# Eight of eighteen transposed blocks moved from DMA to TensorE in 20 attention steps, and one weight scaling moved from GpSimd to ScalarE

## The chip, the core and the metric

The kernel runs on one core of a Trainium2 chip. Its engines are TensorE (PE; PEld for its weight loads), VectorE (DVE), ScalarE (ACT), GpSimd (POOL) and SyncE (SP), which here only issues DMAs. Each engine works through its own queue in order. The metric is the device time of one launch in microseconds; lower is better. Each comparison gives the median of several runs.

## What is computed

Attention with a learned relative bias over 4 batches, 8 heads, 576 positions and head size 64, then two MoE-like dense layers on the 2304 tokens of width 512:

```python
scores = scale * q @ k.T + bias            # bias from log distances through a small MLP
attn = exp(scores - max) / (sum + 1e-9)
x = attn @ v                               # tokens x 512
h = x @ w_in                               # 512 -> 1024
ln = layernorm(h * softmax(h)) * g_ln
x = ln @ w_out                             # 1024 -> 512
gate, val = sigmoid(x @ w_gate), x @ w_val # 512 -> 1536
out = (gate * val) @ w_out2                # 1536 -> 512
```

All products run in float16 on TensorE with each operand split into a high half (the value rounded to float16) and a low half (what the rounding left), so that three float16 products make up one of nearly float32.

## The kernel before

**Attention steps.** The attention is cut into 72 steps (`ticks`). A step takes one pair of heads and 128 query rows (64 of each of two batches in the "M" blocks) against all 576 keys. The first 16 steps are the first block of batches 0 and 1, steps 16 to 19 their "M" block. The loop at the end of the listing runs over t and sends out, for each t, pieces of several steps:

- `a_qk(t)` (L543 to L558): scores on TensorE, into one PSUM tile `score`.
- `a_soft(t)`: VectorE adds the bias and takes the row maximum (L577), ScalarE takes the exponential with its row sum (L584).
- `a_split(t-1)`: the probabilities `pp` (float32, 2 heads x 576) are cast to float16, the high half, by ScalarE (L595) or, in every fourth step, by VectorE (L593); GpSimd subtracts to get the low half (L596 for 512 columns, L598 for the remaining 64); then one DMA issued by SP (L601) transposes the whole tile `p16`, 18 blocks of 128x128, into `pt`, so that the keys lie on the partitions. The trace calls the tile `p16` by the name p.
- `a_pv(t-4)`: TensorE multiplies the blocks of `pt` with V (L620, 28 matmuls; 56 in an "M" step). `a_x` and `a_xt` scale by the row sums and transpose the result for the first MoE.

The rings that bear on it: `p16` has 2 buffers until the first MoE's pools open and 3 after that (`NP160`, `NP16`); `p` and `pt` have 3, then 4. The PSUM pool "m" has 4 buffers, which the bias tiles, K and Q transposes, `a_xt` and the first MoE share.

**Side work.** Beside the steps run small pieces of side work, five for each t at first, then three: decoding, measuring and splitting of the first MoE's weights (`w1_steps`: L183 to L192, L717, L697 to L699), the bias tables for the later blocks (L403, L456, L476, L482, stored to `bias_d`), and then the first MoE itself (L767 to L832). After some 87 pieces, at about t = 17, `open_moe` runs, and from the t after that TensorE's order is as the code writes it (`tc.manual_schedule`); ahead of that, and on the other engines, a planner places the instructions by estimated times, the attention's with a higher priority.

**Second MoE.** Its three weight matrices are decoded (L183 to L188), and each block of 128x512 goes through `split_w`: GpSimd multiplies by a power of two into `w2tmp` (L695, two buffers), ScalarE casts the high half (L698), GpSimd subtracts to the low half (L699). The third matrix (12 blocks) can start when `w2_scale_out` has found its scale (L1148), and its halves are used by `second_out` (L1372). Beside this VectorE makes sums of blocks of the first two matrices (`w2_sums`, L1228) for the products that follow (L1304), and `gate_val` (L1342 to L1348, with L1209 and L1210) runs the gates of the first two groups of tokens.

## Time and profile before

| | us |
|---|---|
| median of 3 runs | 1077.29 (1076.18 to 1077.48) |
| the profiled execution, its own time | 1073.33 |
| its span, first to last instruction | 1071.6 |
| TensorE busy | 898.8 (84%) |
| VectorE busy | 769.3 (72%) |
| ScalarE busy | 618.9 (58%) |
| GpSimd busy | 426.4 (40%) |

The attention steps start at 72 us and end at about 570 us. Steps 0 to 19 take until about 250 us. From 570 to about 790 us the second MoE's weights are made ready beside the last tiles of the first MoE and the first two groups of the second; from 809 us on only products of the second MoE are left. In the rows below, "x" is the count, times are us from the start of the span unless marked ns, "[1.41 <-ACT ...]" is the idle time of the engine ahead of the instruction and what ended it, and 128x512 f16<-128x512 f32 is the shape of the output and of the input.

### The profile page before, as it was taken

The page shows a single profiled execution, that of the slowest core. Times are in us where ns is not written, and L with a number is a line of the kernel's source. Part 1 is how long each engine was busy: PE and PEld are TensorE (multiplying, and loading weights), DVE is VectorE, ACT ScalarE, POOL GpSimd, SP SyncE. Part 2 cuts the span into 40 slices and gives each one's busy share as a digit, 9 for nine tenths or more (in the row PEclk, how much of TensorE's full clock was granted, in tenths as well). Part 3 has the DMA queues.
Part 4 walks back from the last instruction along what each step waited for, and adds up shares of the span by engine and source line. Part 5 has one row for each costly group of instructions (what it writes and reads, how often), then busy time and mean ns, then how long its engine had stood idle before and what let it go on. Part 6 is the DMA issues. An engine that isn't in the chain of part 4 may idle for free.

```text
span 1071.6 us, 23952 instructions
## 1 busy us (share of the span) xinstructions
PE 898.8 (84%) x9566; PEld 634.6 (59%) x9566; DVE 769.3 (72%) x1556; ACT 618.9 (58%) x1283; POOL 426.4 (40%) x386
## 2 busy tenths in 40 slices
PE   2656465668888789989998887798999999999998
PEld 2534344455665566667665664345577856866873
DVE  6879989885576676667664999999954762871760
ACT  4787684767677797778873677744342322331331
POOL 3357555565566666455640487567000000000000
PEclk9656675568899999999999999998999999999999
DMA  7878999899889899999964555500110010001001
GB/s 226 286 231 201 219 242 274 201 239 197 171 177 204 181 196 200 194 205 204 162 123 152 165 158 186 168 24 17 40 40 20 1 60 20 2 1 41 2 1 40
DMA packets 256576, 146.54 MB, mean 137 GB/s; under 512 B 215376, under 2 KB 230992, under 8 KB 256464
## 3 DMA queue, kind: packets, MB, share of 16 engines
q1 hardware_dynamic: 253888, 143.18, 56.4%
q0 software_dynamic: 2048, 1.58, 0.6%
q8 instruction: 75, 1.23, 0.5%
q10 hardware_dynamic: 528, 0.26, 0.1%
q14 instruction: 37, 0.30, 0.1%
HBM read 82.46 MB, written 20.05 MB: 96 GB/s over the span
## 4 chain that ended last, share of the span: by engine, by line
PE 30%; DVE 12%; DMA 3%; issue 2%; POOL 2%; ACT 2%; SPq 0%; POOLq 0%; DVEq 0%; ACTq 0%
PE prod L1304 15%; PE ops L1372 10%; DVE fs L1228 3%; DVE w2f L185 2%; DMA wraw<-in_moe_w_gate_dram 2%; DVE w2f L188 2%; PE x2ps L824 2%; DMA wraw<-in_moe_w_val_dram 1%; POOL w2tmp L695 1%; PE s_ps L1342 1%; PE hps L767 1%; DVE w2s L1228 1%; POOL w2f L699 1%; DVE w2f L184 1%; DMA wraw<-in_moe_w_out_dram 1%
## 5 line engine op out<-in xcount | busy, mean ns | idle before, releaser
L596 POOL TENSOR_TENSOR p<-p,p 128x1024 f16<-128x1024 f32 x72 | 156.2, 2170 | 132.6 <-ACT p L595 89.9
L1228 DVE TENSOR_TENSOR fr<-prod,fr 128x512 f32<-128x512 f32 x126 | 85.0, 687 | 93.8 <-PE prod L1304 92.1
L1372 PE MATMUL ops<-w2f,gv 128*128 128x512 f16 x648 | 144.0, 381 | 4.4 <-POOL w2f L699 2.2
L584 ACT ACTIVATE p<-p,m,sc 128x576 f32<-128x576 f32 x144 | 124.1, 864 | 2.6
L824 PE MATMUL x2ps<-lt,w1f 128*128 128x128 f16 x1728 | 110.0, 224 | 13.9 <-DVE lt L813 11.7
L577 DVE CUSTOM_DVE_ANT_0 p<-score,gk 128x576 f32<-128x576 f32 x144 | 102.9, 750 | 20.9 <-PE score L558 19.3
L824 PEld LDWEIGHTS <-w1f 128*128 128x128 f16 x1728 | 104.3, 100 | 20.9 <-issue 18.6
L1342 PE MATMUL s_ps<-xb,w2f 128*128 128x512 f16 (+1 forms) x576 | 99.9, 332 | 12.7 <-DVE fr L1348 11.2
L1372 PEld LDWEIGHTS <-gv 128*128 128x128 f16 x648 | 63.5, 98 | 79.0 <-issue 5.9
L620 PE MATMUL xps<-gk,pt 128*128 128x64 f16 (+1 forms) x2240 | 88.9, 204 | 17.3 <-DMA pt<-p 17.2
L456 PEld LDWEIGHTS <-mask 128*128 128x128 f16 (+1 forms) x1312 | 65.9, 122 | 55.4 <-issue 20.6
L620 PEld LDWEIGHTS <-pt 128*128 128x128 f16 (+1 forms) x2240 | 83.3, 108 | 25.6 <-DMA pt<-p 18.9
L1304 PEld LDWEIGHTS <-w2f 128*128 128x128 f16 x864 | 84.5, 98 | 11.8 <-issue 1.1
L1342 PEld LDWEIGHTS <-w2f 128*128 128x128 f16 x576 | 57.5, 100 | 53.4 <-issue 11.6
L553 PE MATMUL score<-gk,qt 64*128 64x512 f16 (+1 forms) x480 | 71.0, 429 | 19.8 <-DVE m L577 8.5
L1209 ACT ACTIVATE gv<-fr 128x512 f16<-128x512 f32 (+1 forms) x60 | 34.8, 585 | 84.5 <-DVE fr L1362 70.4
L456 PE MATMUL bp<-rhs,mask 128*128 128x64 f16 (+1 forms) x960 | 53.1, 225 | 29.3 <-DVE gb L482 15.5
L767 PE MATMUL hps<-w1f,xt 128*128 128x512 f16 x312 | 72.6, 379 | 3.1 <-DVE mm L778 1.9
L595 ACT ACTIVATE p<-p 128x1152 f16<-128x1152 f32 x54 | 62.6, 1160 | 11.2 <-DMA pt<-p 9.3
L1304 PEld LDWEIGHTS <-w2s 128*128 128x128 f16 x648 | 63.4, 98 | 7.3
L582 ACT ACTIVATE m<-m,sc 128x1 f32<-128x1 f32 x144 | 40.0, 288 | 46.0 <-DVE m L577 45.7
L767 PEld LDWEIGHTS <-xt 128*128 128x128 f16 x384 | 36.7, 99 | 46.8 <-issue 9.9
(196 smaller groups left out, 1796.8 us busy)
## 6 DMA issues: line engine op xcount, KB each, us to landing
gk<-bias_d SPq DMA_DIRECT2D x24, 576.0 KB
wraw<-in_moe_w_out_dram SPq DMA_DIRECT2D x20, 512.0 KB
wraw<-in_moe_w_gate_dram SPq DMA_DIRECT2D x12, 512.0 KB
wraw<-in_moe_w_val_dram SPq DMA_DIRECT2D x12, 512.0 KB
sraw<-in_q_dram SPq DMA_DIRECT2D x12, 384.0 KB
sraw<-in_k_dram SPq DMA_DIRECT2D x12, 384.0 KB
sraw<-in_v_dram SPq DMA_DIRECT2D x12, 384.0 KB
bias_d<-gk SPq DMA_DIRECT2D x8, 576.0 KB
```

The lines of the kernel that those rows point to most:

```text
L456: pe.matmul(big[0:np_, jj // 8, o:o + 64], lhsT, rhs[i].rearrange("p c h g -> p (c h g)"), start=(i == 0), stop=(i == 1),)
L553: pe.matmul(score[p0:p1, 1024 * hh:1024 * hh + 512], qt[rows, nr * ql + r, p0:p1], KT[bb, hp][rows, 640 * kl:640 * kl + 512], start=(m == ...
L577: dve.tensor_tensor_reduce(out=pp[:, hh], in0=score[:, 960 * hh:960 * hh + S], in1=bi, scale=1.0, scalar=-3.0e38, op0=ALU.add, op1=ALU.max ...
L584: act.activation(out=pp[:, hh], in_=pp[:, hh], func=ACTF.Exp, bias=m[:, 2 + hh:3 + hh], scale=col(C), accum_out=sm[:, c + hh:c + hh + 1])
L596: pool.tensor_tensor(out=p16[:, :, 640:1152], in0=view(pp, 0, [[640, 2], [1, 512]]), in1=view(p16, 0, [[1280, 2], [1, 512]]), op=ALU.subtract)
L620: pe.matmul(o, a, b_, start=(n == 0), stop=(n == len(seq) - 1))
L767: pe.matmul(h, xt[:, xl, kk, off:off + 128], win16[:, 2 * kk + n, wl], start=(kk == 0 and xl == 0 and wl == 0), stop=(kk == 3 and xl == 1),)
L824: pe.matmul(ps[:, dc], wout16[:, f, wl, 128 * dc:128 * dc + 128], lt[:, ll, f], start=(n == 0), stop=(n == 23))
L1228: dve.tensor_tensor(out=out_, in0=a, in1=b, op=op)
L1304: pe.matmul(p[:, jf, 0:nn], w(wl, kk, jf), x(xl, kk), start=(m == 0), stop=(m == 5))
L1342: pe.matmul(ps[:, 0:n], w[:, 4 * (j // 4) + c, wl, o:o + 128], xx[:, 0:n, c, xl, :], start=(m == 0), stop=(m == 11))
L1372: pe.matmul(ps, gvs[j // 4][:, gl, j % 4, 128 * tt:128 * tt + 128], w2h16[2][:, j, wl], start=(m == 0), stop=(m == 35))
```

## The change

Two independent edits.

In the first 20 steps (`NPE`) the DMA transposes only the first 10 of 18 blocks: the high halves and the 64-column tails. For that the tile `p16` is laid out anew, the two 512-column low halves behind everything else. The other 8 blocks, the low halves, are transposed by TensorE against a float16 identity (`id16`) into one PSUM tile of pool "m", and ScalarE copies them into the rest of `pt` (`a_lo`, called for step t-2 behind `a_split(t-1)`). Steps 20 to 71 transpose all 18 blocks by DMA as before, in the new layout; `pv_seq` numbers its blocks accordingly.

In the second MoE the scaling of the third matrix goes from GpSimd (L695) to ScalarE; the cast and the subtraction stay where they are.

```diff
--- before.py
+++ after.py
@@ -74,6 +74,7 @@
 MLEAD = 2
 LAG_PV = 4
 LAG_X = 1
+NPE = 20
 
 
 def TQ(nc):
@@ -136,6 +137,7 @@
 
     ones_sb = const.tile([128, 128], F32, name="ones_sb")
     id_sb = const.tile([128, 128], F32, name="id_sb")
+    id16 = const.tile([128, 128], F16, name="id16")
     sc = const.tile([128, 32], F32, name="sc")
     gs = const.tile([128, 8], F32, name="gs")
     nhalf = const.tile([128, 1], F32, name="nhalf")
@@ -587,28 +589,44 @@
 
     def a_split(i):
         pp = st2.pop(i)
-        p16 = ring("p16", [128, 2, 1152], F16)
-        hi = view(p16, 0, [[1216, 2], [1, S]])
+        p16 = ring("p16", [128, 2304], F16)
+        hi = view(p16, 0, [[704, 2], [1, S]])
+        lo = p16[:, 1280:2304].rearrange("p (r c) -> p r c", r=2)
         if i % 4 in HI_DVE:
             dve.tensor_copy(hi, pp)
         else:
-            act.activation(out=hi, in_=pp, func=ACTF.Copy)
-        pool.tensor_tensor(out=p16[:, :, 640:1152], in0=view(pp, 0, [[640, 2], [1, 512]]),
-                           in1=view(p16, 0, [[1280, 2], [1, 512]]), op=ALU.subtract)
-        pool.tensor_tensor(out=view(p16, 576, [[576, 2], [1, 64]]), in0=view(pp, 512, [[64, 2], [1, 64]]),
-                           in1=view(p16, 512, [[704, 2], [1, 64]]), op=ALU.subtract)
-        pt = ring("pt", [128, 2, 9, 128], F16)
-        trs[i] = sp.dma_start_transpose(out=pt.rearrange("p r c q -> p (r c) q"), in_=p16.rearrange("p r c -> p (r c)"))
+            glob["hi"] = act.activation(out=hi, in_=pp, func=ACTF.Copy)
+        pool.tensor_tensor(out=lo, in0=view(pp, 0, [[640, 2], [1, 512]]),
+                           in1=view(p16, 0, [[768, 2], [1, 512]]), op=ALU.subtract)
+        pool.tensor_tensor(out=view(p16, 576, [[64, 2], [1, 64]]), in0=view(pp, 512, [[64, 2], [1, 64]]),
+                           in1=view(p16, 512, [[192, 2], [1, 64]]), op=ALU.subtract)
+        pt = ring("pt", [128, 18, 128], F16)
+        n = 10 if i < NPE else 18
+        trs[i] = sp.dma_start_transpose(out=pt[:, 0:n], in_=p16[:, 0:128 * n])
         st3[i] = pt
+        if i < NPE:
+            los[i] = lo
+
+    los = {}
+
+    def a_lo(i):
+        if i not in los:
+            return
+        lo, pt = los.pop(i), st3[i]
+        ps = ps_m.tile([128, 2, 4, 128], F16, name="plo", tag="m")
+        for hh in range(2):
+            for c in range(4):
+                pe.transpose(ps[:, hh, c], lo[:, hh, 128 * c:128 * c + 128], id16)
+        act.activation(out=pt[:, 10:18], in_=ps.rearrange("p h c q -> p (h c) q"), func=ACTF.Copy)
 
     def pv_seq(vt, hh, lhs):
         seq = []
         for c in range(5):
-            b_ = (c + hh) % 5
+            b_ = 5 * hh + (c + hh) % 5
             seq.append((lhs(b_), vt[:, hh, c]))
             seq.append((lhs(b_), vt[:, hh, 5 + c]))
         for c in range(4):
-            seq.append((lhs(5 + c), vt[:, hh, c]))
+            seq.append((lhs(10 + 4 * hh + c), vt[:, hh, c]))
         return seq
 
     def a_pv(i):
@@ -624,7 +642,7 @@
             for hh in range(2):
                 for par in range(2):
                     po = slice(64 * par, 64 * par + 64)
-                    run(pv_seq(VT[2 * bp + par, hp], hh, lambda c: pt[:, hh, c, po]),
+                    run(pv_seq(VT[2 * bp + par, hp], hh, lambda c: pt[:, c, po]),
                         x[po, 64 * hh:64 * hh + 64])
             xps[bp, qd, hp, bset] = x
         else:
@@ -634,7 +652,7 @@
             x = xps[key]
             for hh in range(2):
                 o = 256 * bset.index(b) + 128 * r + 64 * hh
-                run(pv_seq(VT[2 * bp + b, hp], hh, lambda c: pt[:, hh, c, :]), x[:, o:o + 64])
+                run(pv_seq(VT[2 * bp + b, hp], hh, lambda c: pt[:, c, :]), x[:, o:o + 64])
 
     def a_x(i):
         bp, qd, hp, r, b, bset = ticks[i]
@@ -690,8 +708,8 @@
         sp.dma_start(out=raw.rearrange("p f t -> p (f t)"), in_=src[rows, cols].bitcast(I32))
         return raw
 
-    def split_w(w, s_, hi, lo, tmp, eng=None):
-        if eng is None:
+    def split_w(w, s_, hi, lo, tmp, eng=None, scaler=None):
+        if eng is None and scaler is None:
             pool.tensor_scalar(out=tmp, in0=w, scalar1=s_, scalar2=0.0, op0=ALU.mult, op1=ALU.add)
         else:
             act.activation(out=tmp, in_=w, func=ACTF.Copy, scale=s_)
@@ -965,6 +983,7 @@
     bs["mid"] = load_mid(bs["sign"])
     ck = stats(flat(k), SW)
     sp.dma_start(out=id_sb, in_=ident)
+    pool.tensor_copy(id16, id_sb)
     load_q((0, 0, 0, 0))
     load_raw(k, 0, 0, "k")
     with tc.high_priority(1000):
@@ -1070,6 +1089,7 @@
                 a_soft(t)
             if 0 <= t - 1 < nticks:
                 a_split(t - 1)
+            a_lo(t - 2)
             if 0 <= t - LAG_PV - LAG_X < nticks:
                 a_x(t - LAG_PV - LAG_X)
         if t % 2 == 0 and 2 <= t < 16:
@@ -1126,7 +1146,8 @@
 
     def w2_split(mat, jc, c):
         split_w(w2f[mat][:, 4 * jc + c], sw[:, jc, S_G + mat:S_G + mat + 1], w2h16[mat][:, 4 * jc + c, 0],
-                w2h16[mat][:, 4 * jc + c, 1], w2t_p.tile([128, 512], F32, name="w2tmp", tag="w2sgn"))
+                w2h16[mat][:, 4 * jc + c, 1], w2t_p.tile([128, 512], F32, name="w2tmp", tag="w2sgn"),
+                scaler=act if mat == 2 else None)
 
     def w2_scale(jc):
         pow2(w2st, [(4 * jc, 4 * jc + 4)], sw[:, jc, P_G:P_G + 1], sw[:, jc, S_G:S_G + 1], psx[0], 13)
```

## Rows read from the trace of the kernel before

**Rows 1.** Busy us (x instructions) by engine, TensorE's clock, DMA share, GB/s, by stage.

```profile
85.00:190.00 105.00, 63.08 (x898) 48.33 (x896) 100.26 (x187) 72.43 (x159) 60.44 (x55) 0.66 1.00 236
190.00:262.00 72.00, 51.90 (x736) 36.41 (x737) 51.98 (x128) 50.59 (x115) 41.12 (x31) 0.71 0.93 216
262.00:570.00 308.00, 275.99 (x3936) 201.68 (x3933) 200.79 (x508) 236.66 (x521) 178.31 (x158) 0.97 0.92 178
705.00:748.00 43.00, 35.65 (x183) 19.29 (x182) 42.25 (x53) 17.24 (x32) 36.88 (x24) 0.88 0.08 25
748.00:809.00 61.00, 60.16 (x382) 37.19 (x380) 44.82 (x82) 23.48 (x46) 0.00 (x0) 1.00 0.12 40
```

**Rows 2.** Waits, 85 to 262 us: who for whom, us in total, times, longest.

```profile
ACT p L595 <- DMA pt<-p: 9.3, 7, 3.4
...
DVE w1f L184 <- ACT w1f L183: 2.1, 4, 1.3
...
DVE xtm L684 <- ACT xtm L683: 0.3, 1, 0.3
```

**Rows 3.** Timeline of the SP queue: transposes of steps 8, 15, 18 to 20.

```profile
157.77 3.09 SPq L601 DMA_TRANSPOSE pt<-p  x1
...
219.44 5.08 SPq L601 DMA_TRANSPOSE pt<-p  x1
...
251.27 10.45 SPq L601 DMA_TRANSPOSE pt<-p  x3
```

**Rows 4.** Timeline of ScalarE, TensorE and VectorE: casts that wait, and behind them.

```profile
164.20 1.16 ACT L595 ACTIVATE p<-p 128x1152 f16<-128x1152 f32 x1 [3.39 <-DMA pt<-p]
...
166.88 1.03 PE L553 MATMUL score<-gk,qt 64*128 64x512 f16 x4 [1.41 <-ACT qt L292]
...
228.16 0.76 DVE L593 CAST p<-p 128x1152 f16<-128x1152 f32 x1 [3.49 <-DMA pt<-p]
...
260.91 0.76 DVE L593 CAST p<-p 128x1152 f16<-128x1152 f32 x1 [2.61 <-DMA pt<-p]
```

**Rows 5.** Groups by shape, 262 to 560 us (busy, mean ns), and two timeline rows of TensorE.

```profile
L595 ACT ACTIVATE p<-p 128x1152 f16<-128x1152 f32 x38 | 44.1, 1160 | 1.9 <-issue 0.4
L812 ACT ACTIVATE lt<-ltp 128x512 f16<-128x512 f32 x24 | 13.6, 584 | 0.0
...
121.93 1.09 PE L251 MATMUL ktp<-id_sb,kv 128*128 128x128 f32 x4 [0.92 <-DMA kv<-in_k_dram]
...
283.00 5.17 PE L824 MATMUL x2ps<-lt,w1f 128*128 128x128 f16 x47 [2.96 <-DVE lt L813]
```

**Rows 6.** Groups by shape on GpSimd, 705 to 743 us.

```profile
L695 POOL TENSOR_SCALAR w2tmp<-w2f,sw 128x512 f32<-128x512 f32 x12 | 18.7, 1570 | 18.7 <-DVE sw L1148 18.7
L699 POOL TENSOR_TENSOR w2f<-w2tmp,w2f 128x512 f16<-128x512 f32 x12 | 18.4, 1555 | 0.0
```

**Rows 7.** Waits, 705 to 750 us.

```profile
PE s_ps L1342 <- DVE fr L1348: 3.0, 2, 2.3
PE ops L1372 <- POOL w2f L699: 2.2, 2, 1.5
PE ops L1372 <- ACT w2f L698: 2.1, 2, 1.7
```

**Rows 8.** Timeline of GpSimd and VectorE side by side.

```profile
708.68 3.14 POOL L699 TENSOR_TENSOR w2f<-w2tmp,w2f 128x512 f16<-128x512 f32 x2
711.81 2.85 POOL L695 TENSOR_SCALAR w2tmp<-w2f,sw 128x512 f32<-128x512 f32 x2
...
710.74 1.64 DVE L1228 TENSOR_TENSOR w2s<-fs,w2s 128x512 f16<-128x512 f32 x1
712.30 0.68 DVE L1228 TENSOR_TENSOR fs<-fs 128x512 f32<-128x512 f32 x1
```

**Rows 9.** Timeline: end of step 20's scores, end of step 18's low half.

```profile
245.43 0.34 PE L558 MATMUL score<-gk,qt 128*128 128x128 f16 x3
...
250.81 0.43 POOL L598 TENSOR_TENSOR p<-p,p 128x128 f16<-128x128 f32 x1
```

## The prediction

> **What bounds the kernel now.** Start with the table of stages [rows 1] and ask in each which engine has no room. From 85 to 190 us VectorE is busy 100.26 of 105 us; this is where the first attention steps run together with the decoding of the first MoE's weights and the bias tables. From 190 to 262 us nobody is full: VectorE 52 of 72, TensorE 52, ScalarE 51. In both stretches the DMA engines are as good as full (share 1.00 and 0.93). From 262 to 570 us TensorE takes over (276 of 308), and from 748 to the end it has no gap at all (60.16 of 61 in the stretch shown). Between them lies a knot at 705 to 748 us: VectorE 42.25 of 43, GpSimd 36.88, TensorE only 35.65. So time can be gained at two places, which are those that the diff touches: the waits among engines in 85 to 262 us, and the 7.35 us in which TensorE stands between 705 and 748 us. What is gained at either place moves everything behind it, since from 262 on the attention steps, then the decoding of the second MoE, then TensorE follow each other without slack; I count a microsecond there as a microsecond at the end.
>
> Second view: who waits for whom in 85 to 262 us [rows 2]. The casts of the probabilities wait for DMA pt<-p: on ScalarE (L595) 9.3 us, on VectorE (L593) twice, 3.49 and 2.61 us [rows 4], 15.4 in all. The reason is in the code: p16 has two buffers here, so the cast of step i must wait until the transposing DMA of step i-2 has read its buffer. Third view, the DMA queue's timeline beside it: the transpose of step 8 (one a step, counted on SP) is issued at 157.77 and holds the SP queue 3.09 us [rows 3], and the cast of step 10 starts at 164.20, 6.4 us after that start, having held ScalarE idle for 3.39 us [rows 4]; step 15 (219.44, 5.08 us of issue) lets go of VectorE's cast of step 17 at 228.16, after 8.7 us.
>
> **Part 1, the first 20 steps.** Each DMA transpose goes from 18 to 10 blocks of 128x128. If issue and flight both go by the number of blocks, 6.4 us become 3.6 and 8.7 become 4.8; if they go by the instruction, nothing is gained. I take the former, because the 10.45 us of three transposes in a row [rows 3] and the full DMA engines look like work by the byte; at the 3.48 us of that row SP's queue then loses 20 x 3.48 x 8/18 = 31 us of issue, and the loads of weights, K, V and Q that stand behind it start earlier. Not every wait is on the path. I follow three, for which the rows show what stands behind them [rows 4]: ScalarE's 3.39 us, behind which the query's copy (L292) waits, and behind that the scores of step 12 (PE 166.88, idle 1.41 for that copy); VectorE's own 3.49 us at 228.16; VectorE's own 2.61 us at 260.91, the cast of step 21, which stands behind three transposes issued in a row, two of which get shorter. With 2.8 us less of waiting in the first (6.4 - 3.6) and all of the second (8.7 - 4.8 is more than 3.49) and third: 2.8 + 3.5 + 2.6 = 8.9 us. The casts' other waits, six on ScalarE, lie in stretches where VectorE is full anyway; they would be another 5.9 at most (9.3 - 3.4).
>
> What is added. TensorE: 8 transposes of 128 columns in float16 a step. Nearest row: 47 matmuls of 128 columns took 5.17 us at the lower clock, 110 ns each; four float32 transposes took 1.09 us, 270 ns each [rows 5]. So 0.9 to 2.2 us a step, 18 to 44 us in 20 steps; I take 0.9, float16 against float16. TensorE stands 62 of the 177 us [rows 1], so this lies beside VectorE's work. ScalarE: one copy of 128x1024 a step. The cast of 128x1152 took 1.16 us, the copy of 128x512 out of PSUM 0.584 us [rows 5]: 1.03 to 1.17, I take 1.05, 21 us in all. ScalarE is busy 123 of 177 us and goes to 144. VectorE's idle time that ScalarE ended is 8.8 us in 12 waits, from L184 (2.1 us, 4) to L684 xtm (0.3, 1) [rows 2]. A step is 8.9 us long and holds one copy; if a copy counts where it stands within the last 2.5 us ahead of such a wait, that is 12 x 0.28 x 1.05 = 3.5 us given back. Bounds: 0, and 12 x 1.05 = 12.6. The copy id16 is one small cast on GpSimd long before its first use; GpSimd's and VectorE's work for the steps is otherwise the same in count and shape, so I cost it at nothing. Each step also takes one of the four PSUM buffers "m" from the bias groups for the length of 8 transposes and a copy, some 2 of 8.9 us; VectorE is what those groups wait for, so I leave it at nothing, and it belongs to the slower rival. Part 1: 8.9 - 3.5 = 5.4 us gained.
>
> The Trainium skill, VectorE: DVE Perf Modes, section The three transpose paths, puts a 128x128 transpose at 390 ns on TensorE and 1309 ns by DMA, and advises TensorE where PSUM will do. The Trainium skill, TensorE: Matmul & The Clock Gate, section Part 4: PE-mode transpose, gives about 275 ns inside a kernel. By that figure the eight blocks would be 2.2 us a step, 44 us in all, an estimate from that page that agrees with the upper bound above and would still fit TensorE's idle time; no row here shows a float16 transpose.
>
> **Part 2, the third weight matrix of the second MoE.** Before, GpSimd scales (L695, 12 x 1.57 = 18.7 us) and subtracts (L699, 12 x 1.56 = 18.4 us) [rows 6] back to back, 37.1 us. After, ScalarE scales (12 instructions of 128x512 like L812, 0.58 us each [rows 5], 7.0 us, and it is busy 17.24 of 43 [rows 1]), and GpSimd only subtracts: the last weight is ready some 18 us earlier. TensorE's waits for just these weights, 2.2 us for GpSimd L699 and 2.1 us for ScalarE L698 [rows 7], go: 4.3 us. Next late is VectorE: TensorE already waits 3.0 us for its gate product (L1348) [rows 7], and VectorE's sums are slowed by GpSimd: 1.64 us at 710.74, while GpSimd subtracts (708.68 to 711.82), but 0.68 us at 712.30, while it scales (711.81 to 714.66) [rows 8]. So the slow partner is the subtraction, which stays, and stands denser. Bounds: 7.35, all that TensorE stands, if VectorE is freed under the scaling too; and below nothing, -2.9, if each of three gate products comes behind one more slowed sum (3 x 0.96) and nothing else is won. I take 4.3, the waits that the row names.
>
> The Trainium skill, SBUF — State Buffer, section Who interferes with whom, says that a VectorE instruction with two SBUF inputs blocks against any GpSimd instruction that reads SBUF. By that rule taking the scaling away would free VectorE under both, and the gain would be the upper bound; the rows above show the full slowing under the subtraction alone, so I stay with 4.3.
>
> **Sum.** The profiled execution took 1073.33 us (span 1071.6), 4 us under the median of the runs, 1077.29. I take the difference as the same for both kernels: 1077.3 - 5.4 - 4.3 = 1067.6 us.
>
> **Rivals.** (a) *More of the DMA relief counts.* If all 15.4 us of the casts' waits are worth their length, ScalarE's copies cost nothing, and part 2 gives 5 or more: 1077.3 - 15.4 - 5 = 1057. For it: DMA share 1.00. Against it: VectorE's 100.26 of 105. Part 2 alone at 7.35, with VectorE free under the scaling, gives 1077.3 - 5.4 - 7.35 = 1064.6; it lies in the forecast's range, and I give it 0.12 of the forecast's chance. (b) *No change.* VectorE is the bound up to 190 us and what is saved behind it goes into waits for ScalarE, while the gate product takes over in part 2: 1077. (c) *Slower: TensorE waits in its queue for GpSimd's low halves.* From the point where the code fixes TensorE's order (when the first MoE's pools open, about step 18) the transposes of step t-2 stand right behind the scores of step t, ahead of everything else. In the trace the scores of step 20 end at 245.77, and the low half of step 18 is finished on GpSimd only at 251.24 [rows 9]: 5.5 us in which TensorE would stand, with its scores of step 21 and the first MoE behind it. That occurs once or twice (steps 18 and 19 alone lie behind that point); in the steps before it, a placement by an estimate can do the same. Two such stalls, the upper cost of ScalarE's copies (12.6) and the gains of 8.9 and 4.3: 1077.3 + 11 + 12.6 - 8.9 - 4.3 = 1087.7; one stall and a middle cost of 8 for the copies: 1077.3 + 5.5 + 8 - 8.9 - 4.3 = 1077.6, so it decides from the second stall on. I take the middle of the two, 1082. That the change does not do what it says I rule out: the diff shortens the DMA's own operands.
>
> **How the numbers follow.** Forecast (1063 to 1074) 0.50; (a) 0.16; (b) 0.12; (c) 0.22. For 8 in 10 the range takes most of (a) and the typical case of (c): 1057 to 1082. This kernel's runs agree to about 0.2%, 2 us. Faster by more than that: the forecast and (a), 0.66; within it 0.12; slower 0.22.
>
> **What would show it.** Right: waits of L595 and the DVE cast for DMA pt<-p under 5 us together; transposes on SP about 2 us in the first 20 steps; the scores of step 20 done 4 to 6 us ahead of 245.8; GpSimd's twelve L699 on this matrix within 25 us instead of 37; TensorE's wait for w2f gone and its idle time in that stretch about 3 us. Wrong: if the SP issue stays above 3 us, the transpose goes by the instruction; if the scores of step 20 come later, ScalarE's queue or the PSUM buffers ate the gain; if TensorE shows a wait of 4 us or more for GpSimd's p16 at the new transposes, it is (c); if VectorE's idle time in 85 to 262 us does not shrink, VectorE was the bound and it is (b).

## The result and the profile after

The changed kernel takes 1083.98 us (median of 4 runs, 1082.88 to 1085.29), the kernel before on the same chip 1076.74: ratio 1.0072, 95% interval 1.0051 to 1.0093. It is 0.7% slower, where 1067.6 was forecast, and it lies 2 us above the range (1057 to 1082). Its profiled execution has a span of 1081.5 us against 1071.6.

The stages of the changed kernel, with the columns of [rows 1]; the last two are moved by the 14 us by which the second MoE begins later:

```profile
85.00:190.00 105.00, 56.08 (x825) 42.85 (x823) 91.14 (x181) 79.29 (x165) 57.10 (x54) 0.73 0.84 212
190.00:262.00 72.00, 49.20 (x855) 37.77 (x854) 52.19 (x120) 55.42 (x112) 42.21 (x32) 0.82 0.76 175
262.00:570.00 308.00, 274.49 (x3814) 198.58 (x3813) 200.74 (x505) 237.66 (x525) 172.96 (x154) 0.96 0.93 175
719.00:762.00 43.00, 38.17 (x216) 21.74 (x215) 42.93 (x61) 27.19 (x48) 20.68 (x12) 0.96 0.09 31
762.00:823.00 61.00, 60.20 (x391) 38.08 (x390) 41.88 (x76) 22.18 (x43) 0.00 (x0) 1.00 0.11 40
```

The DMA share fell as meant (1.00 to 0.84, 0.93 to 0.76), ScalarE took on 7 us in the first row, VectorE is busy 9 us less there, and GpSimd's 36.88 us of the knot are 20.68. Yet no step came earlier. Waits of the same kernel from 85 to 262 us (engine, tile and line waited for: us in total, times, longest), and its groups in that stretch:

```profile
POOL p L599 <- ACT p L598: 21.0, 8, 7.1
...
ACT pt L620 <- PE plo L619: 13.4, 9, 4.3
...
PE plo L619 <- POOL p L599: 8.7, 1, 8.7
```

```profile
L620 ACT ACTIVATE pt<-plo 128x1024 f16<-128x1024 f16 x19 | 19.3, 1016 | 13.4 <-PE plo L619 13.4
L598 ACT ACTIVATE p<-p 128x1152 f16<-128x1152 f32 x15 | 17.4, 1158 | 0.0
L619 PE MATMUL plo<-id,p 128*128 128x128 f16 x160 | 16.2, 260 | 21.5 <-DVE gb L484 9.2 <-POOL p L599 8.7 <-DVE gk L257 3.5
```

The casts no longer wait for the DMA at all ([rows 2] had 9.3 us on ScalarE); now GpSimd waits 21.0 us for the casts, and TensorE once 8.7 us for GpSimd. That one wait, in the timelines of TensorE, GpSimd and ScalarE:

```profile
246.04 0.34 PE L560 MATMUL score<-gk,qt 128*128 128x128 f16 x3
255.12 1.03 PE L619 MATMUL plo<-id,p 128*128 128x128 f16 x8 [8.74 <-POOL p L599]
256.08 2.64 PE L638 MATMUL xps<-gk,pt 128*64 128x64 f16 x56
258.65 1.09 PE L684 MATMUL xtp<-id_sb,xn 128*128 128x128 f32 x4
259.67 0.82 PE L555 MATMUL score<-gk,qt 64*128 64x512 f16 x6
...
250.47 2.13 POOL L599 TENSOR_TENSOR p<-p,p 128x1024 f16<-128x1024 f32 x1 [1.17 <-ACT sums L668]
252.94 2.13 POOL L599 TENSOR_TENSOR p<-p,p 128x1024 f16<-128x1024 f32 x1
...
249.18 1.15 ACT L598 ACTIVATE p<-p 128x1152 f16<-128x1152 f32 x1
251.18 1.16 ACT L598 ACTIVATE p<-p 128x1152 f16<-128x1152 f32 x1
```

TensorE ends step 20's scores at 246.04 + 0.34 = 246.38 (245.77 by [rows 9]) and stands until GpSimd's second subtraction ends, at 252.94 + 2.13 = 255.07. The scores of step 21 (259.67) stand behind the transposes in TensorE's order; the trace lists nothing else that they wait for. The Trainium skill, PSUM — Partial Sum Buffer, section Engine vs sequencer instructions, says that matmuls start and complete in program order; the trace agrees, nothing passes the waiting transposes in 8.74 us.

Where the time goes between the two traces is read from the first row of each step's softmax on VectorE (L577 before, L579 after), the last small instruction of the second MoE's scales (VectorE, col(CO) in w2_scale_out), and the first product of the last stage (TensorE "prod"); behind that product all kernels here take 262.3 us. The experiments stand in the same table, in us. Each row is one traced execution and not the median of its kernel; that of "sums last, part 2" took 1057.4 us against a median of 1066.54.

| kernel | step 20 | step 21 | step 24 | step 71 | scales | product | from scales to product |
|---|---|---|---|---|---|---|---|
| before | 245.9 | 249.1 | 274.1 | 550.4 | 705.3 | 809.2 | 104.0 |
| after | 246.5 | 261.4 | 283.0 | 566.1 | 719.4 | 819.2 | 99.9 |
| part 2 alone | 242.6 | 245.8 | 270.2 | 548.8 | 701.6 | 801.8 | 100.2 |
| part 1 alone | 252.4 | 266.5 | 288.0 | 571.0 | 724.1 | 828.0 | 103.9 |
| both, 18 steps | 248.5 | 251.9 | 276.3 | 553.8 | 710.6 | 810.4 | 99.8 |
| relief alone, part 2 | 248.3 | 252.3 | 274.1 | 552.0 | 706.2 | 806.0 | 99.8 |
| no transposes on TensorE, part 2 | 248.8 | 252.0 | 275.8 | 552.4 | 709.2 | 809.4 | 100.2 |
| cost alone, part 2 | 255.4 | 259.5 | 279.0 | 555.7 | 710.4 | 803.4 | 93.0 |
| third p16 buffer, part 2 | 259.3 | 263.3 | 285.5 | 563.5 | 716.2 | 816.0 | 99.8 |
| sums last, part 2 | 245.6 | 248.8 | 272.5 | 549.4 | 701.6 | 793.3 | 91.7 |
| sums last, both, 18 steps | 250.7 | 254.7 | 279.7 | 555.0 | 707.3 | 799.5 | 92.2 |
| sums last, before | 249.1 | 252.3 | 276.7 | 555.9 | 708.6 | 801.6 | 93.0 |

After against before: +0.6 at step 20, +12.3 at step 21, +8.8 at step 24, +14.1 at the scales, +10.0 at the product. How much one trace can tell is seen from five rows whose attention steps do the same work on every engine (before, part 2 alone, no transposes, sums last with part 2, sums last with before): step 24 lies between 270.2 and 276.7, step 71 between 548.8 and 555.9. A shift of 3 us there is no finding; 8.74 us in one idle interval is.

The second part, in the groups of the knot (719 to 764 us) and its waits:

```profile
L717 POOL TENSOR_TENSOR w2f<-w2tmp,w2f 128x512 f16<-128x512 f32 x12 | 20.7, 1737 | 32.4 <-ACT w2f L716 22.6 <-DVE fs L1249 9.6
L715 ACT ACTIVATE w2tmp<-w2f,sw 128x512 f32<-128x512 f32 x12 | 8.5, 717 | 1.0 <-POOL w2f L717 0.8
```

```profile
ACT w2s L1252 <- DVE fs L1249: 12.4, 6, 5.2
POOL w2f L717 <- DVE fs L1249: 9.6, 3, 4.2
...
PE s_ps L1363 <- DVE fr L1369: 4.7, 2, 3.7
```

TensorE's waits for the weights of [rows 7] are gone, but the twelve subtractions stretch over 721.5 to 753.7 us, 32 us instead of the "within 25" of the prediction: a ScalarE scale or cast stands behind a cast w2s that waits for VectorE's sum. TensorE's wait for the gate product (L1348 before, L1369 here) is 4.7 us instead of 3.0.

### The profile page after: what moved, and what is told of

It is laid out like the page before. It is cut to its first block, busy times and chain, and to the rows that moved or that the text cites. A ratio compares the mean times of both kernels' runs of the same rounds, so it can differ in the third digit from the quotient of the medians.

```text
span 1081.5 us, 24319 instructions
## 1 busy us (share of the span) xinstructions
PE 899.0 (83%) x9726; PEld 637.2 (59%) x9726; DVE 763.8 (71%) x1556; ACT 645.5 (60%) x1315; POOL 407.2 (38%) x375
## 4 chain that ended last, share of the span: by engine, by line
PE 36%; DVE 9%; DMA 3%; issue 2%; ACT 1%; SPq 0%; DVEq 0%; ACTq 0%
PE prod L1325 15%; PE ops L1393 12%; PE s_ps L1363 4%; DVE fs L1249 2%; PE x2ps L842 2%; DVE w2f L187 2%; DMA wraw<-in_moe_w_gate_dram 2%; DVE w2f L190 1%; DMA wraw<-in_moe_w_val_dram 1%; PE hps L785 1%; DVE w2f L186 1%; PE xps L638 1%; DVE w2s L1249 0%; DVE fr L1369 0%; DVE e L809 0%
## 5 line engine op out<-in xcount | busy, mean ns | idle before, releaser
L842 PE MATMUL x2ps<-lt,w1f 128*128 128x128 f16 x1728 | 113.6, 228 | 13.9 <-DVE lt L831 11.2
L842 PEld LDWEIGHTS <-w1f 128*128 128x128 f16 x1728 | 107.9, 103 | 21.9 <-issue 19.4
L579 DVE CUSTOM_DVE_ANT_0 p<-score,gk 128x576 f32<-128x576 f32 x144 | 103.0, 752 | 20.5 <-PE score L560 20.1
L1363 PE MATMUL s_ps<-xb,w2f 128*128 128x512 f16 (+1 forms) x576 | 102.1, 336 | 11.2 <-DVE fr L1369 9.6
L638 PE MATMUL xps<-gk,pt 128*128 128x64 f16 (+1 forms) x2240 | 84.3, 198 | 12.5 <-DMA pt<-p 5.7
L638 PEld LDWEIGHTS <-pt 128*128 128x128 f16 (+1 forms) x2240 | 78.9, 104 | 20.3 <-issue 7.0
L458 PEld LDWEIGHTS <-mask 128*128 128x128 f16 (+1 forms) x1312 | 58.7, 113 | 39.7 <-issue 20.7
L555 PE MATMUL score<-gk,qt 64*128 64x512 f16 (+1 forms) x480 | 68.7, 411 | 15.7 <-DVE m L579 7.6
L717 POOL TENSOR_TENSOR w2f<-w2tmp,w2f 128x512 f16<-128x512 f32 x36 | 55.8, 1562 | 35.9 <-ACT w2f L716 26.0
```

Source lines behind the costliest of these rows:

```text
L555: pe.matmul(score[p0:p1, 1024 * hh:1024 * hh + 512], qt[rows, nr * ql + r, p0:p1], KT[bb, hp][rows, 640 * kl:640 * kl + 512], start=(m == ...
L579: dve.tensor_tensor_reduce(out=pp[:, hh], in0=score[:, 960 * hh:960 * hh + S], in1=bi, scale=1.0, scalar=-3.0e38, op0=ALU.add, op1=ALU.max ...
L638: pe.matmul(o, a, b_, start=(n == 0), stop=(n == len(seq) - 1))
L842: pe.matmul(ps[:, dc], wout16[:, f, wl, 128 * dc:128 * dc + 128], lt[:, ll, f], start=(n == 0), stop=(n == 23))
L1363: pe.matmul(ps[:, 0:n], w[:, 4 * (j // 4) + c, wl, o:o + 128], xx[:, 0:n, c, xl, :], start=(m == 0), stop=(m == 11))
```

## The experiments

Ratios are to runs of the kernel before on the same chip, interleaved with each group; its medians were 1074.6 to 1076.4 us.

**The two parts, and two ways around the stop.** Part 2 alone is the kernel before with the scaler in split_w; part 1 alone is the changed kernel with

```
-                scaler=act if mat == 2 else None)
+                scaler=None)
```

> Part 2 alone (third matrix scaled by ScalarE, attention as before). Theory: the two parts add, and part 2 is the gain of 4.1 us seen between the scale's end and the first product (104.0 us before, 99.9 after): 4 us faster than before, about 1073. Rival: part 2's gain depends on what ScalarE and GpSimd have left over after part 1, or it is the loss itself: no gain, or slower than before.

> Part 1 alone (transposes split, scaling on GpSimd as before). Theory: the whole loss lies in part 1, 15.6 us at the last attention step, of which a little may come back: 11 to 14 us slower than before, and some 4 us slower than both parts together. Rival (the parts do not add): within 3 us of the changed kernel.

Measured: part 2 alone 1069.07 us, ratio 0.9958 [0.9937, 0.9979]; part 1 alone 1091.67, 1.0145 [1.0113, 1.0176], with the same stop at step 18 (8.06 us). The loss is all part 1's; part 2 gives 0.4%, about what it was priced at. Part 1 alone lies 7.8 us above the changed kernel where 4 were expected; the intervals leave room for that. Then the stop is taken out, by 18 steps instead of 20 (NPE = 18), or by transposing a step later (a_lo(t - 3)):

> Both parts, but only 18 steps instead of 20 have their low halves transposed by TensorE, so that steps 18 and 19, whose transposes stand in the written order close behind the scores of steps 20 and 21, go by DMA. Theory (TensorE stands 8.7 us at step 18's transposes, waiting for GpSimd): the stand is gone, step 21 starts within 3 us of the kernel before, and the time falls by 9 to 13 us against the changed kernel, to about 1072, faster than before. Rival (ScalarE's copies and PSUM buffers cost it all along, or the planner's order): two steps of twenty less, so at most 2 us faster than the changed kernel.

> Both parts, 20 steps, the transposes of the low halves called for step t-3 instead of t-2, one step later in TensorE's written order, with the same work. Theory (it is the place in the queue): TensorE's stand of 8.7 us at step 18 falls under 2 us, and the time by 7 to 13 us, to about 1073. Rival (it is the added work): no change, within 2 us of the changed kernel; or later transposes hold back the products with V.

Measured: 18 steps 1073.1, ratio 0.999 [0.9967, 1.0012]; a step later 1077.23, 1.0017 [0.9997, 1.0036]. Timeline of TensorE at the same place, of the kernel with 18 steps and (from 249.73) of the other:

```profile
247.28 0.82 PE L555 MATMUL score<-gk,qt 64*128 64x512 f16 x6
248.04 0.34 PE L560 MATMUL score<-gk,qt 128*128 128x128 f16 x3
248.31 1.66 PE L638 MATMUL xps<-gk,pt 128*64 128x64 f16 x56
```

```profile
249.73 0.34 PE L560 MATMUL score<-gk,qt 128*128 128x128 f16 x3
250.81 0.62 PE L619 MATMUL plo<-id,p 128*128 128x128 f16 x8 [0.74 <-POOL p L599]
251.35 1.66 PE L638 MATMUL xps<-gk,pt 128*64 128x64 f16 x56
```

With 18 steps the ratio is 0.0082 under that of the changed kernel, 8.8 us; a step later it is 0.0055, 5.9 us, a little less than the 7 to 13 expected. Each of the two figures is uncertain by some 3 us. TensorE's stop was 8.74 us, and both kernels take it away, the second with all the added work still in place: so the stop is the slowdown, and most or all of it reaches the end. Part 1 without the stop still stands 3 to 4 us behind part 2 alone, with intervals that overlap, where the prediction had it 5.4 us ahead.

**Where the relief went.** Relief alone: as the changed kernel, but no transposes on TensorE and no copies: it leaves the low halves of these steps out and reads high blocks in their place, with

```
+    def blk(i, c):
+        return c - 10 if i < NPE and c >= 10 else c
-                    run(pv_seq(VT[2 * bp + par, hp], hh, lambda c: pt[:, c, po]),
+                    run(pv_seq(VT[2 * bp + par, hp], hh, lambda c: pt[:, blk(i, c), po]),
...
-            a_lo(t - 2)
```

The base is NPE = 0. Cost alone is NPE = 18 with

```
-        n = 10 if i < NPE else 18
-        trs[i] = sp.dma_start_transpose(out=pt[:, 0:n], in_=p16[:, 0:128 * n])
+        trs[i] = sp.dma_start_transpose(out=pt, in_=p16)
...
-        act.activation(out=pt[:, 10:18], in_=ps.rearrange("p h c q -> p (h c) q"), func=ACTF.Copy)
+        act.activation(out=scr, in_=ps.rearrange("p h c q -> p (h c) q"), func=ACTF.Copy)
```

> The relief alone: in the first 20 steps the DMA transposes 10 of the 18 blocks, and nothing takes over the other 8 (no TensorE transposes, no ScalarE copies). The transposition of the low halves of the first 512 columns is left out in these steps; the weighting of the values reads high blocks in their place, so every matmul is still issued. Part 2 is in. Beside it stands the kernel in which all 18 blocks go by DMA in the new layout, with part 2. Theory A, the relief is worth what the prediction took (8.9 us) and the added work on ScalarE and TensorE eats it: this kernel lies 5 to 9 us below that one, ratio to before about 0.988 to 0.991, and step 21 starts 5 us or more earlier than before. Theory B, the waits of the casts for the DMA were not on the path, VectorE and the written order of the planner were: within 2 us of that kernel, ratio 0.994 to 0.998, step 21 within 2 us of before, although the casts' waits for DMA pt<-p shrink to under 5 us.

> All 18 blocks by DMA in every step, in the new layout of p16 and pt, with part 2. The base for the other two. Both theories: as the kernel with part 2 alone, ratio 0.994 to 0.998, since the layout of p16 and pt changes no count and no shape that an engine sees. If it is 3 us or more slower than that (ratio 0.999 or above), the layout or the order that the planner makes of it is itself the cost, and the loss between the part-2 kernel and the one with 18 steps lies there.

> The cost alone: the DMA transposes all 18 blocks in every step, and in the first 18 steps TensorE transposes 8 of them as well and ScalarE copies them to a tile that nobody reads. 18 steps, so that the stop of TensorE at step 18 is out. Part 2 is in. Theory A: the cost of 18 copies and transposes with no relief is 5 to 9 us, ratio to before 1.000 to 1.005, clearly above the kernel with 18 steps and both (0.999). Theory B: the cost is the 3 to 4 us by which the kernel with 18 steps stands behind part 2 alone, and taking the relief away changes nothing: ratio 0.997 to 1.001, within 2 us of that kernel.

> Both parts, TensorE's transposes in the first 16 steps. No stop of TensorE at step 18 is possible. Theory A and B alike: between the kernel with 18 steps (0.999) and part 2 alone (0.996), 1070 to 1074 on a chip with before at 1074.6. If it falls under part 2 alone by 2 us or more, the relief is worth something in the early steps and the cost sits in steps 16 and 17.

Measured: relief alone 1072.08, ratio 0.9975 [0.9951, 0.9999]; base 1073.63, 0.9965 [0.994, 0.999]; cost alone 1067.94, 0.9924 [0.9895, 0.9952]; 16 steps 1076.39, 1.0007 [0.9987, 1.0026]. The stage 85 to 190 us of the base, of relief alone and of cost alone (columns of [rows 1]):

```profile
85.00:190.00 105.00, 63.04 (x884) 46.83 (x881) 99.44 (x184) 70.77 (x155) 63.02 (x56) 0.66 1.00 238
```

```profile
85.00:190.00 105.00, 62.42 (x894) 47.33 (x894) 99.50 (x183) 69.50 (x152) 57.82 (x53) 0.67 0.90 215
```

```profile
85.00:190.00 105.00, 62.12 (x862) 49.20 (x864) 92.24 (x178) 76.83 (x161) 56.89 (x53) 0.66 1.01 232
```

The relief frees a tenth of the DMA engines and leaves VectorE at 99.5 of 105 us, and the steps come no earlier. The casts' waits for the DMA are 13.9 us in the base (9.9 on ScalarE, 4.0 on VectorE) and 7.9 with the relief (4.2 and 3.7); in cost alone, which has no relief, there is no such wait at all; on ScalarE the copies stand between the casts there, and the casts come later (a reading, not tested by itself). These waits are slack: they shrink when the DMA is faster and also when the casts are slower, and the relief moves step 24 only from 275.8 to 274.1, inside the scatter. Relief alone lies 0.0010 above its base, uncertain by some 0.0035 (3.7 us), which excludes a gain of 8.9 us: theory B has the time right. Two of its signs missed, since the waits are not under 5 us and step 21 comes 3.2 us after that of the kernel before. 16 steps came out some 2 us above what was expected; that stays unexplained. Neither theory had cost alone as the fastest kernel; the table shows where: its steps are no earlier (step 71 at 555.7, base 552.4), and it wins 7 us between scales and product (93.0 against 100.2). That is the second MoE, not the transposes.

A third p16 buffer (NP160 = 3, with part 2 alone) takes the casts' waits away by another means:

> Part 2 alone, with three p16 buffers instead of two in the steps before the first MoE's pools open. A cast then waits for the transpose of step i-3 and not of step i-2, and nothing else is touched. Theory A, the casts' waits for the DMA (15.4 us in the profile before) are worth the 8.9 us that the prediction took: ratio 0.986 to 0.990. Theory B, those waits are not on the path: they shrink to under 5 us and the ratio stays at part 2 alone, 0.994 to 0.998, step 21 within 3 us of before.

Measured: 1083.96, ratio 1.0072 [1.0047, 1.0098], some 12 us worse than part 2 alone; both theories missed the time. The casts' waits went from 14.4 us (8.3 and 6.1) to 3.4, and then, at step 18:

```profile
ACT p L595 <- DMA pt<-p: 3.4, 2, 2.1
```

```profile
251.91 0.76 DVE L577 CUSTOM_DVE_ANT_0 p<-score,gk 128x576 f32<-128x576 f32 x1 [6.55 <-POOL w1f L699]
```

The planner wrote another order, in which step 18 waits for the last split of the first MoE's weights. So this run does not price the waits alone; it shows that removing them and reordering can cost more than they were worth.

**The order in the second MoE.** In cost alone VectorE's sums of the weights (w2_sums) begin at 731.1, behind the last subtraction at 730.9, and the twelve subtractions take 18 us. Three kernels were to have that order on purpose, through

```
-        (eng or pool).tensor_tensor(out=lo, in0=tmp, in1=hi, op=ALU.subtract)
+        glob["sub"] = (eng or pool).tensor_tensor(out=lo, in0=tmp, in1=hi, op=ALU.subtract)
...
-    with tc.issue_after(glob["so"].ins):
+    with tc.issue_after(glob["sub"].ins):
```

> Part 2 alone, and the sums of the second MoE's weights (VectorE, line w2_sums) may be issued only behind the last of the twelve subtractions, where the cost-only kernel had them. Theory O, the order on ScalarE and GpSimd is what kept the twelve splits at 32 us: they take 18 to 20 us here, the end of the scales to the first product takes 93 us (part 2 alone 100.2, before 104.0), and the ratio is 0.987 to 0.991. Rival, the cost-only kernel was fast through its first 20 steps: the time stays at part 2 alone, 0.994 to 0.998.

> The kernel before with the sums issued behind the last subtraction, GpSimd scaling as well as subtracting. Theory O: the twelve pairs keep GpSimd for 37 us, so the sums start some 37 us behind the scales and the first product comes 37 + 72 = 109 us behind them instead of 104: ratio 1.003 to 1.007. The order pays only with ScalarE's scaling. Rival, the late sums pay by themselves, since VectorE is no longer slowed by GpSimd: ratio 0.990 to 0.996.

> Both parts with TensorE's transposes in 18 steps, and the sums behind the last subtraction. Beside the kernel with part 2 alone and the same order it shows what part 1 is worth without the stop of TensorE at step 18. Theory, part 1 costs 2 to 4 us even so: ratio 0.990 to 0.994, 2 to 4 us above that kernel. Rival, the 4 us between 18 steps and part 2 alone lay in the order of the second MoE: no difference between the two.

Measured: 1074.48, ratio 0.9991 [0.9966, 1.0017]; 1078.36, 1.0021 [1.0002, 1.0039]; 1076.27, 1.0005 [0.9983, 1.0027]. The edit did the opposite: a bound to an instruction of GpSimd did not hold VectorE's sums, and the old bound to one of VectorE was gone. The first sums ran at 702.68 in the first of them and its scales ended at 723.6, 22 us later than with part 2 alone (this traced execution took 1084.79 us, 10 above the median); in the other two the scales come at 722.2 and 719.9, 17 and 9 us later than in the kernel before and with 18 steps. These three tell nothing of the order that was meant. The next three have it, by one column that VectorE copies from the last subtraction's output:

```
+    tick = const.tile([128, 1], F32, name="tick")
...
     with tc.issue_after(glob["so"].ins):
+        glob["tick"] = dve.tensor_copy(tick, w2h16[2][:, 11, 1, 0:1])
+    with tc.issue_after(glob["tick"].ins):
         for jc in range(3):
```

> Part 2 alone, with one VectorE copy of a single column that reads the last of the twelve subtractions, and the sums of the weights in VectorE's order behind it. In the three runs before this one the order was asked for on GpSimd, which binds nothing on VectorE, and taking the old bound away let sums go ahead of the scales (first product 97 us behind the scales, but the scales 22 us later). Theory O, the order of the sums and the splits is what made the cost-only kernel fast: twelve splits in 18 to 20 us, scales to first product 93 us instead of 100.2, ratio 0.987 to 0.991. Rival, that kernel was fast for another reason: ratio 0.994 to 0.998.

> Both parts with TensorE's transposes in 18 steps, and the same order of the sums. Against the kernel with part 2 alone and that order it gives the worth of part 1 without the stop of TensorE. Theory B, part 1 costs 2 to 4 us: ratio 0.990 to 0.995. Rival A, the relief shows once the second MoE is in order: the same or lower than part 2 alone with that order, 0.985 to 0.990.

> The kernel before, GpSimd scaling and subtracting, with the sums behind the last subtraction. Theory O: the pairs keep GpSimd for 37 us, the first product comes 37 + 72 = 109 us behind the scales instead of 104: ratio 1.003 to 1.007, so the order pays only with ScalarE's scaling. Rival, late sums pay by themselves since GpSimd no longer slows VectorE: 0.990 to 0.997.

Measured: with part 2 alone 1066.54, ratio 0.9902 [0.9868, 0.9937]; both parts, 18 steps 1064.19, 0.9898 [0.9869, 0.9927]; the kernel before with nothing but this order 1065.33, 0.99 [0.9872, 0.9927]. All three lie 1% below the kernel before. The order itself is worth 1.0% in that kernel, 0.9% with both parts in 18 steps (from 0.999) and 0.6% with part 2 alone (from 0.9958), and the expectation that it pays only with ScalarE's scaling was wrong. Groups on GpSimd of the last one, 705 to 750 us, beside [rows 6], and one group of VectorE's sums of before and of that kernel:

```profile
L700 POOL TENSOR_TENSOR w2f<-w2tmp,w2f 128x512 f16<-128x512 f32 x12 | 14.5, 1231 | 0.4
L696 POOL TENSOR_SCALAR w2tmp<-w2f,sw 128x512 f32<-128x512 f32 x12 | 9.2, 775 | 19.0 <-DVE sw L1149 19.0
```

```profile
L1228 DVE TENSOR_TENSOR fs<-w2f 128x512 f32<-128x512 f16 x24 | 20.3, 879 | 0.0
```

```profile
L1229 DVE TENSOR_TENSOR fs<-w2f 128x512 f32<-128x512 f16 x24 | 15.6, 684 | 0.0
```

Apart, GpSimd scales in 0.78 us instead of 1.57, subtracts in 1.23 instead of 1.56, and VectorE sums in 0.68 instead of 0.88. The twelve pairs take 24 us instead of 37, and from the scales to the product it is 93.0 us instead of 104.0: 11 us, for no instruction moved to another engine. That stretch before and in that kernel (columns of [rows 1]):

```profile
705.30:809.20 103.90, 95.51 (x562) 56.29 (x561) 86.80 (x131) 40.62 (x77) 36.88 (x24) 0.95 0.10 34
708.60:801.60 93.00, 91.89 (x568) 55.42 (x567) 74.05 (x132) 40.80 (x77) 23.58 (x24) 1.00 0.09 35
```

Of the 11 us, 7.3 are idle time of TensorE that went (8.4 to 1.1), and 3.6 are its own busy time for the same products, at a mean granted clock of 0.95 before and of 1.00, the upper of its two levels throughout (2.4 GHz), with the order. Two things change at once: GpSimd and VectorE no longer slow each other, and VectorE's gate products no longer stand among the sums in its queue. No run separates the two. With the order in place part 2 (0.9902 against 0.99) and part 1 without its stop (0.9898 against 0.9902) make no difference that these runs can tell.

**Why the stop was 8.7 and not 5.5 us.** In GpSimd's list of instructions in the kernel before, by buffer number, the subtractions of step 19 (buffer 3773) stand ahead of those of step 18 (buffer 3711, taken earlier); the changed kernel has the same swap.

```
97 L596 TENSOR_TENSOR p_3773<-p,p_3773 128x2x512
98 L598 TENSOR_TENSOR p_3773<-p,p_3773 128x2x64
99 L596 TENSOR_TENSOR p_3711<-p,p_3711 128x2x512
100 L598 TENSOR_TENSOR p_3711<-p,p_3711 128x2x64
```

One run binds step 19's subtractions behind step 18's (with tc.issue_after(subs[18].ins), on GpSimd itself):

> The changed kernel, with GpSimd's subtractions of step 19 bound behind those of step 18 in GpSimd's own order. In the kernels before and after, GpSimd's list has step 19's pair of subtractions ahead of step 18's. Theory, that is why TensorE's stop at step 18 was 8.74 us and not the 5.5 that the prediction priced: the pair of step 19 (2.13 + 0.43 us) stands ahead of the one TensorE waits for. The stop shrinks to 5.5 to 6.7 us, step 21 starts 2 to 3 us earlier than in the changed kernel against step 20, ratio 1.003 to 1.007. Rival, the subtraction of step 18 waits for its cast anyway, which ScalarE gives behind step 19's exponentials: the stop stays at 8 to 9 us, ratio 1.006 to 1.009.

Measured: 1083.18, ratio 1.006 [1.0037, 1.0084]. The stop is 7.54 us, 1.2 less; by its interval the time is not told apart from that of the changed kernel. Timelines of TensorE, ScalarE and GpSimd:

```profile
257.38 1.03 PE L621 MATMUL plo<-id,p 128*128 128x128 f16 x8 [7.54 <-POOL p L600]
...
251.98 1.15 ACT L598 ACTIVATE p<-p 128x1152 f16<-128x1152 f32 x1
253.13 0.85 ACT L586 ACTIVATE p<-p,m,sc 128x576 f32<-128x576 f32 x1
...
253.98 1.15 ACT L598 ACTIVATE p<-p 128x1152 f16<-128x1152 f32 x1
...
255.20 2.12 POOL L600 TENSOR_TENSOR p<-p,p 128x1024 f16<-128x1024 f32 x1 [3.12 <-ACT p L598]
```

Both theories have a share: ScalarE too casts step 19 (251.98) ahead of step 18 (253.98, behind an exponential), so GpSimd, now in the right order, waits for the second cast. One pair of subtractions (252.94 - 250.47 = 2.5 us in the changed kernel) is most of the 3.2 us between the 5.5 read and the 8.74 of the stop.

The order on ScalarE may weigh more than that. In the changed kernel the rows of step 18 on VectorE are at 233.84, those of step 19 at 243.79, and the last exponential of step 18 is this one:

```profile
237.91 0.86 ACT L586 ACTIVATE p<-p,m,sc 128x576 f32<-128x576 f32 x1
```

It ends at 238.77, and the cast of step 18 begins at 251.18, 12.4 us later, with other work of ScalarE and the cast of step 19 (249.18) ahead of it. So, as far as the trace shows, the operand that TensorE stood for was late by the order of ScalarE's work. Whether that cast could have gone earlier, and why the planner ordered the two steps so, was not tried.

## Why the prediction was wrong

Two terms make up the miss of 16.4 us (1083.98 less 1067.6), of about the same size: the sum left out TensorE's stop, 8.7 us, and it counted 8.9 us for the relief. Either alone would have left the time inside the range.

**TensorE's stop: rival (c) was named, but left out of the sum, and sized and weighed wrongly.** Its place (steps 18 and 19, behind TensorE's scores), its mechanism and its sign in the trace ("a wait of 4 us or more for GpSimd's p16 at the new transposes") are what happened, once. The size came from [rows 9], whose subtraction at 250.81 was taken for step 18's. It was step 19's; step 18's pair is the next one in the trace of before:

```profile
248.72 2.14 POOL L596 TENSOR_TENSOR p<-p,p 128x1024 f16<-128x1024 f32 x1 [0.98 <-POOL w1f L699]
250.81 0.43 POOL L598 TENSOR_TENSOR p<-p,p 128x128 f16<-128x128 f32 x1
251.20 2.13 POOL L596 TENSOR_TENSOR p<-p,p 128x1024 f16<-128x1024 f32 x1
```

251.20 + 2.13 = 253.33, less 245.77 = 7.6 us; measured 8.74. It also should not have been a chance of 0.22: the order that puts the transposes there is in the code, and the two times were in one trace. The rival's rule that it "decides from the second stall on" hung on a gain of 8.9 us for the relief; without that gain one stall decides.

**Part 1, the relief: 8.9 us priced, none found.** The base and relief alone differ by 0.1% in the wrong direction, inside their intervals. The transposes on SP did become short (1.35 to 3.1 us; the changed kernel's last three, two of them short, 8.70 against the 10.45 of [rows 3]), and the casts' waits went, as the prediction asked for. The wrong step was to count a wait at full length because a row showed what stood behind it ([rows 4]). With the waits gone, nothing behind them came earlier; that it waited for VectorE or for the written order instead is a reading that no run shows by itself. Rival (b) had this half right, and its sign came true: VectorE's idle time in 85 to 262 us did not shrink, it grew from 24.8 to 33.7 us.

**Part 1, the cost.** The copy took 1.02 us (1.05 priced), eight transposes 0.81 us (16.2 / 20; 0.9 priced). Kernels with them (18 steps, 16 steps, cost alone, sums last with 18 steps) reach step 71 at 553.8 to 556.7, those without at 548.8 to 555.9; by the means, 555.3 and 551.5, the cost is about 4 us (3.5 priced). The two groups overlap, one more trace with 18 steps (the first attempt at the order) reaches step 71 at 549.2, and with the sums last no cost shows at the end, so the 4 us are not shown.

**Part 2: right in size, in part by luck.** Priced 4.3; the knot became 4.1 us shorter (104.0 to 99.9), and part 2 alone measured 0.42%, 4.5 us. The waits for the weights went as priced, but the wait for the gate product grew by 1.7 us, so that TensorE's idle time from the scales to the product fell by 2.8 (8.4 to 5.6); the other 1.3 us came from its busy time (95.5 to 94.2), at a mean granted clock of 0.95 and 0.98, which the prediction did not price. The subtractions did not close up to 25 us. And the bound of 7.35 was within reach, by the order and not by moving the scale: the idle time fell to 1.1 in the kernels with the sums last. The prediction read [rows 8] as "the slow partner is the subtraction". That was VectorE's side alone; the scale's 1.57 us was itself twice its own length, and that side was not priced. The Trainium skill, SBUF — State Buffer, section Who interferes with whom, says that a VectorE instruction with two SBUF inputs contends with GpSimd instructions that read SBUF, and that issue order decides who is blocked. The means agree for both engines (0.88 to 0.68, 1.57 to 0.78). By that rule the subtraction, which stays on GpSimd, contends too, so the prediction's reading, that moving the scale would free VectorE under both, does not follow from it.

**The sum again with what was measured:** 1077.3 + 8.7 (stop) + 4 (cost, not shown) - 0 (relief) - 4.1 (part 2) = 1085.9, against 1083.98. Part 1 alone came out at +15.6 us where these terms give 12.7; the 3 us more are of the size of the scatter. From step 24 to 71, in code that did not change, the traces of the changed kernel and of part 1 alone take 283.1 and 283.0 us and all others 274.9 to 279.2, the run of the last experiment, which has the stop too, among them (279.0); this stays unexplained.

## What to carry to other kernels

Work put into an engine's queue takes over every wait of its producers: before moving it, find in the trace when its operand is finished, follow the buffer and not the next row of the same line, and compare that with when the queue arrives there. Ask also whether the operand is late by the work ahead of it or only by the order on a third engine. A wait in front of an engine is a gain only if the work behind it has nothing else to wait for; making the resource faster in one run and its user slower in another shows slack at once. And two engines that slow each other should be priced on both sides: here, putting them one behind the other gave 1% in the kernel before, more than either move of work.

## What the runs showed of the hardware

- GpSimd's scale of 128x512 float32 takes 0.78 us without VectorE's sums beside it (sums last, before) and 1.57 with them (before); its subtraction 1.16 to 1.23 (cost alone; sums last, before) and 1.56 to 1.74 (before; after); a sum on VectorE 0.68 and 0.88.
- TensorE's granted clock from 190 to 262 us, a mean over stretches at its two levels (1.2 and 2.4 GHz), is 0.71 before, 0.82 after and 0.87 with 18 steps of transposes, while its busy time there is 51.9, 49.2 and 55.8 us of 72, for 736, 855 and 930 matmuls: with the clock higher, more matmuls took less time in the second.
- In the changed kernel TensorE stops once for 1.90 us at 484.54, in the middle of a row of matmuls, with no releaser ("issue"). Nothing here shows what it was.
